# A carried angle added by VectorE to turned gates, in place of a TensorE matmul

## The chip, the cores and the metric

One core of one Trainium2 chip runs the program. The time is the device time of one execution in microseconds (us), given as the median of several executions, with the lowest and highest. A profiled execution is one execution, and its span is some 1.8 us shorter than its own time. In the lines of the profile PE is TensorE, PEld its loading of weights, DVE is VectorE, ACT is ScalarE, POOL is GpSimd, SP is SyncE and SPq its queue. A record is one instruction in the profile. The chain that ended last is the path followed back from the last instruction to whatever released it, step by step.

## The reference, cut to what matters

```python
batch, n_heads, seq, head_dim = 4, 8, 768, 48
n_tokens, d_model, d_ff = 3072, 384, 2048

mag = sqrt(a_re**2 + a_im**2)
a = (a_re + 1j*a_im) * minimum(mag, 0.999) / (mag + 1e-6)      # gates
for t in range(S):                                             # state S, complex
    S = a[t] * S + outer(k[t], v[t])
    y[t] = q[t] @ real(S)
h = x @ w_in                                                   # x: y with heads side by side
out = (h * cos(h)) @ w_out
```

The kernel takes 128 steps as a chunk and two chunks as a group: 24 chunks, 12 groups, six chunks to a batch. Inside a chunk the product of gates over time becomes a running sum of logarithms and of angles, each made by one matmul with a triangular constant. The angle at the end of a chunk is carried into the next one, except where a batch begins (chunks 0, 6, 12, 18).

## The kernel before

`x["tan"]` holds the angles of a group, 128 steps by 2 x 384 columns. The sum `phs` has a second matmul: `last` is zero but for its last row, so it adds the last row of the chunk before, and that row is its carried phase.

```python
def load(g, names, i=None):
    ...
        for i_ in range(G) if i is None else (i,):
            b, c = divmod(g * G + i_, NCH)
            nc.sync.dma_start(out=X[g][name][:, i_],
                              in_=ap[b].rearrange("h (c p) d -> p c h d", p=C)[:, c])

def g_phase(g, i):
    x, n = X[g], g * G + i
    ps = pa.tile([C, DM], F32, tag="a", name="phs")
    first = n % NCH == 0
    matmul(ps, lhsT=turns, rhs=cut(x["tan"], i, 1), start=True, stop=first)
    if not first:
        prev = cut(X[(n - 1) // G]["tan"], (n - 1) % G, 1)
        matmul(ps, lhsT=last, rhs=prev, start=False, stop=True)
    ph = cut(x["tan"], i, 1)
    scalar.copy(out=ph.bitcast(I32), in_=ps)
    vector.tensor_tensor(out=ph, in0=ps, in1=ph.bitcast(I32), op=ALU.subtract)
```

What the steady groups do, in the order in which it is written; the two numbers place a part between the start (0) and the end (1) of a group:

```python
for n in range(2, NG):
    weave((logs(n + 1), 0.0, 0.02), (chunks(n), 0.0, 0.36), (second(n - 1, 0), 0.0, 0.38),
          (prods(n + 1), 0.38, 0.39), (each(g_angle, n + 1), 0.39, 0.4),
          (second(n - 1, 1), 0.4, 0.56), (phases(n + 1), 0.49, 0.51),
          (keys(n + 1), 0.52, 0.7), (first(n), 0.56, 1.0),
          (guarded(n - 1, per) if n > 3 else [], 0.1, 0.9))
```

`first` makes `hp` (x @ w_in), `second` makes `op` (the product with w_out), `chunks` makes `sc`, `sp` and `yp`, the attention of a group. `keys` ends in `moved`, `kT` and `qT`: keys and queries transposed through memory. (Two senses of one word: "turned" queries are these transposed ones; "turned" gates, below, have their rows moved round by one.)

## Time and profile before

| kernel before | value | read from |
|---|---|---|
| time | 720.84 us (720.14 to 721.88) | 3 executions |
| span of the profiled execution | 716.7 us | page |
| TensorE (PE) busy | 688.3 us, 96% | page, part 1 |
| VectorE (DVE) busy | 393.8 us, 55% | page, part 1 |
| period from one `hp` start to the next, the nine of the steady groups | 53.67 to 56.39 us | timeline of PE |

The period varies with a batch's place: two groups out of three have two carried chunks, the third has one.

### The profile page before, as it was taken

The page shows a single profiled execution, that of the slowest core. Times are in us where ns is not written, and L with a number is a line of the kernel's source. Part 1 is how long each engine was busy: PE and PEld are TensorE (multiplying, and loading weights), DVE is VectorE, ACT ScalarE, POOL GpSimd, SP SyncE. Part 2 cuts the span into 40 slices and gives each one's busy share as a digit, 9 for nine tenths or more (in the row PEclk, how much of TensorE's full clock was granted, in tenths as well). Part 3 has the DMA queues.
Part 4 walks back from the last instruction along what each step waited for, and adds up shares of the span by engine and source line. Part 5 has one row for each costly group of instructions (what it writes and reads, how often), then busy time and mean ns, then how long its engine had stood idle before and what let it go on. Part 6 is the DMA issues. An engine that isn't in the chain of part 4 may idle for free.

```text
span 716.7 us, 9385 instructions
## 1 busy us (share of the span) xinstructions
PE 688.3 (96%) x3614; PEld 524.4 (73%) x3614; DVE 393.8 (55%) x548; ACT 386.3 (54%) x690; POOL 26.1 (4%) x45
## 2 busy tenths in 40 slices
PE   6786999999999999999999999999999999999995
PEld 5675776876876876876886876876886786786773
DVE  4889987255455563663663664654645655631110
ACT  6778873564564574484483583474474375342330
POOL 1012000000000000000000000000000000000000
PEclk9979999999999999999999999999999999999998
DMA  9678626625725745646646655556665572272000
GB/s 265 131 226 265 167 56 160 139 55 123 176 49 129 177 133 122 162 138 143 161 137 145 149 145 122 148 155 133 156 154 133 146 163 56 88 173 70 12 0 28
DMA packets 231730, 94.73 MB, mean 132 GB/s; under 512 B 207982, under 2 KB 220145, under 8 KB 231676
## 3 DMA queue, kind: packets, MB, share of 16 engines
q1 hardware_dynamic: 225324, 68.55, 43.5%
q0 software_dynamic: 5632, 25.17, 10.3%
q8 instruction: 30, 0.49, 0.3%
q10 hardware_dynamic: 720, 0.33, 0.2%
q14 instruction: 24, 0.20, 0.1%
HBM read 69.22 MB, written 24.81 MB: 131 GB/s over the span
## 4 chain that ended last, share of the span: by engine, by line
PE 81%; DMA 3%; DVE 3%; SPq 1%; ACT 1%; issue 0%; DVEq 0%
PE op L661 34%; PE hp L661 28%; PE sc L661 6%; PE yp L661 5%; PE phs L661 3%; PE sp L661 3%; DMA qT<-moved 2%; PE lgs L661 2%; DVE w_out L651 1%; SPq L837 1%; DMA raw<-in_moe_w_out_dram 1%; DVE ks L651 0%; DVE qs L651 0%; DMA moved<-tr 0%; DVE tr L651 0%
## 5 line engine op out<-in xcount | busy, mean ns | idle before, releaser
L661 PE MATMUL op<-w_out,gate 128*128 128x384 f32 x768 | 262.8, 489 | 0.7 <-DVE w_out L651 0.7
L661 PE MATMUL hp<-xT,w_in 128*128 128x256 f32 x1152 | 254.3, 382 | 3.9 <-ACT junk L651 3.3
L661 PEld LDWEIGHTS hp<-xT,w_in 128*128 128x128 f32 x1152 | 220.7, 192 | 38.1 <-ACT junk L651 3.7
L661 PEld LDWEIGHTS op<-w_out,gate 128*128 128x128 f32 x768 | 142.3, 190 | 95.1 <-issue 3.7
L651 DVE TENSOR_TENSOR gate<-hp,gate 128x512 f32<-128x512 f32 x96 | 65.5, 683 | 135.4 <-ACT gate L680 135.4
L651 ACT ACTIVATE junk<-hp 128x512 bf16<-128x512 f32 x96 | 57.2, 596 | 81.7 <-DVE gate L651 81.6
L680 ACT ACTIVATE gate<-hp,half_pi_b 128x512 f32<-128x512 f32 x96 | 65.5, 684 | 41.6 <-PE hp L661 41.6
L661 PEld LDWEIGHTS sc<-qT,kT 96*128 96x128 f32 x384 | 47.6, 192 | 11.0 <-issue 4.0
L651 ACT COPY yT<-yp 48x512 f32<-48x512 f32 x44 | 25.4, 577 | 52.7 <-PE yp L661 52.0
L661 PE MATMUL sc<-qT,kT 96*128 96x128 f32 x384 | 49.3, 277 | 2.7 <-DMA qT<-moved 0.9
L651 DVE SCALAR_TENSOR_TENSOR mag<-Q,lg 128x768 f32<-128x768 f32 (+1 forms) x13 | 11.6, 894 | 66.6 <-ACT Q L680 66.6
L651 ACT CAST tan<-phs 128x384 int32<-128x384 f32 x24 | 11.5, 481 | 64.6 <-PE phs L661 64.6
L651 DVE TENSOR_TENSOR atm<-sc,causal 128x512 f32<-128x512 f32 x48 | 32.9, 686 | 19.3 <-PE sc L661 19.3
L651 ACT ACTIVATE ot<-op 128x384 f32<-128x384 f32 x24 | 11.6, 483 | 48.6 <-PE op L661 48.6
L676 ACT ACT_TABLE_LOAD x26 | 33.4, 1283 | 3.5 <-issue 3.1
L661 PE MATMUL yp<-atm,v 128*48 128x128 f32 x352 | 33.5, 277 | 0.0
L651 DVE TENSOR_TENSOR tan<-phs,tan 128x384 f32<-128x384 f32 x24 | 13.4, 557 | 30.9 <-ACT tan L651 30.9
L661 PE MATMUL sp<-v,ks 128*96 128x48 f32 x320 | 29.6, 245 | 0.0
L661 PE MATMUL yp<-qT,state 96*48 96x128 f32 x304 | 29.6, 272 | 0.0
L661 PEld LDWEIGHTS sp<-v,ks 128*96 128x96 f32 x320 | 29.4, 165 | 0.3 <-issue 0.2
L661 PE MATMUL phs<-tan,turns 128*128 128x384 f32 x48 | 19.6, 492 | 4.3 <-ACT tan L680 4.3
L661 PEld LDWEIGHTS yp<-atm,v 128*48 128x48 f32 x352 | 19.3, 122 | 5.6 <-issue 3.3
(93 smaller groups left out, 677.7 us busy)
## 6 DMA issues: line engine op xcount, KB each, us to landing
moved<-tr SPq DMA_DIRECT2D x20, 768.0 KB
raw<-in_moe_w_in_dram POOLq DMA_DIRECT2D x16, 768.0 KB, 6.1
raw<-in_moe_w_out_dram POOLq DMA_DIRECT2D x16, 768.0 KB, 5.1
kT<-moved SPq DMA_DIRECT2D x40, 192.0 KB
qT<-moved SPq DMA_DIRECT2D x10, 768.0 KB
re<-in_a_re_dram SPq DMA_DIRECT2D x24, 192.0 KB
im<-in_a_im_dram SPq DMA_DIRECT2D x24, 192.0 KB
k<-in_k_dram SPq DMA_DIRECT2D x24, 192.0 KB
```

The costliest lines, as they stand in the source:

```text
L651: ins = getattr(self.engine, op)(**kw)
L661: chain(nc.tensor.matmul(out, **kw), "tensor")
L676: chain(nc.scalar.preload_act_table_set(table))
L680: chain(nc.scalar.activation(func=func, **kw))
L837: nc.sync.dma_start(out=X[g][name][:, ds(i * H, n * H), q4], in_=moved[q4])
```

## The change

The gates of group 2 and of the later groups are loaded turned by one row: partition 127 gets step 0 of the chunk, partition p gets step p+1. The triangular constant is turned in the same way, so the sum is the same. What is carried lies in partition 127 of the chunk before, after its sum, and the element that it must be added to lies in partition 127 too. So VectorE can add it in place, on partitions 96 to 127 with a column `carry` that is pi in row 127 and 0 above (the finished sums are kept in units of pi), and the matmul goes. The loads come in parts of 112, 15 and 1 rows. At the same time the order in a group is changed: the decay products come earlier, and the two phase sums stand further apart and earlier.

```diff
+    sums_np = causal_np, np.roll(causal_np, -1, axis=0)
+    carry_np = np.where(step_np == C - 1, np.float32(math.pi), np.float32(0.0))[:, None]
 ...
+            parts = [(0, C, 0)]
+            if name in ("re", "im") and g >= PEG:
+                parts = [(0, C - 16, 1), (C - 16, C - 1, 1)]
+                nc.sync.dma_start(out=tile_[C - 1:C], in_=steps[0:1])
+            for i_ in range(n):
+                for lo, hi, by in parts:
+                    nc.sync.dma_start(out=tile_[lo:hi, i_], in_=steps[lo + by:hi + by, i_])
 ...
+    carry = constant(carry_np, "carry")
 ...
+    def g_carry(g, i):
+        n, some = g * G + i, ds(C - 32, 32)
+        if g >= PEG and n % NCH:
+            head = cut(X[g]["tan"], i, 1)[some]
+            vector.scalar_tensor_tensor(out=head, in0=before(n)[some], scalar=carry[some],
+                                        in1=head, op0=ALU.mult, op1=ALU.add)
 ...  (in g_phase)
+        early = g < PEG and n % NCH
+        if i:
+            g_carry(g, i)
-        matmul(ps, lhsT=turns, rhs=cut(x["tan"], i, 1), start=True, stop=first)
-        if not first:
-            matmul(ps, lhsT=last, rhs=prev, start=False, stop=True)
+        matmul(ps, lhsT=turns[g >= PEG], rhs=cut(x["tan"], i, 1), start=True, stop=not early)
+        if early:
+            matmul(ps, lhsT=last, rhs=before(n), start=False, stop=True)
 ...  (start)
+    sums.append(constant(sums_np[1], "sums_turned", nc.sync))
+    turns.append(constant(sums_np[1] * np.float32(1.0 / math.pi), "turns_turned", nc.sync))
 ...  (steady groups)
-              (prods(n + 1), 0.38, 0.39), (each(g_angle, n + 1), 0.39, 0.4),
-              (second(n - 1, 1), 0.4, 0.56), (phases(n + 1), 0.49, 0.51),
-              (keys(n + 1), 0.52, 0.7), (first(n), 0.56, 1.0),
+              (prods(n + 1), 0.22, 0.24),
+              (second(n - 1, 1), 0.4, 0.56), (phases(n + 1), 0.4, 0.52),
+              (keys(n + 1), 0.49, 0.66), (first(n), 0.56, 1.0),
```

More of the change, by code (lines that the diff above doesn't have):

```diff
@@ L521, in fast_path, with constant @@
     step_np = np.arange(C)
-    sums_np = (step_np[:, None] <= step_np[None, :]).astype(np.float32)
+    causal_np = (step_np[:, None] <= step_np[None, :]).astype(np.float32)
+    sums_np = causal_np, np.roll(causal_np, -1, axis=0)
     last_np = np.zeros((C, C), np.float32)
     last_np[C - 1] = 1.0
-    def constant(array, name):
+    carry_np = np.where(step_np == C - 1, np.float32(math.pi), np.float32(0.0))[:, None]
+    def constant(array, name, queue=nc.scalar):
         t = consts.tile(list(array.shape), F32, name=name)
-        nc.scalar.dma_start(out=t, in_=nc.inline_tensor(array, name=name + "_const").ap())
+        queue.dma_start(out=t, in_=nc.inline_tensor(array, name=name + "_const").ap())
         return t
@@ L548, in load @@
                                      bufs=2 if name == "v" else 1)
-            for i_ in range(G) if i is None else (i,):
-                b, c = divmod(g * G + i_, NCH)
-                nc.sync.dma_start(
-                    out=X[g][name][:, i_],
-                    in_=ap[b].rearrange("h (c p) d -> p c h d", p=C)[:, c])
+            b, c = divmod(g * G + (i or 0), NCH)
+            one, n = i or 0, G if i is None else 1
+            steps = ap[b].rearrange("h (c p) d -> p c h d", p=C)[:, ds(c, n)]
+            tile_ = X[g][name][:, ds(one, n)]
+            parts = [(0, C, 0)]
[5 more added lines that the diff above has]
+                    nc.sync.dma_start(out=tile_[lo:hi, i_], in_=steps[lo + by:hi + by, i_])
     for names in ("re", "im"), ("k", "q"), "v":
@@ L558, in fast_path @@
     ident = constant(np.eye(C, dtype=np.float32), "ident")
-    sums = constant(sums_np, "sums")
-    turns = constant(sums_np * np.float32(1.0 / math.pi), "turns")
+    sums = [constant(sums_np[0], "sums")]
+    turns = [constant(sums_np[0] * np.float32(1.0 / math.pi), "turns")]
     last = constant(last_np, "last")
-    causal = constant(sums_np * np.float32(0.25), "causal")
+    carry = constant(carry_np, "carry")
+    causal = constant(causal_np * np.float32(0.25), "causal")
     tiny_b = scalar_tile(TINY, "tiny_b")
@@ L666, in busy @@
         for _ in range(count):
-            matmul(ps, lhsT=ident, rhs=sums, start=True, stop=True)
+            matmul(ps, lhsT=ident, rhs=sums[0], start=True, stop=True)
     tables = {AF.Ln: "natural_log_exp_and_others", AF.Exp: "natural_log_exp_and_others",
@@ L743, in p_powers @@
         ps = pa.tile([C, DM], F32, tag="a", name="lgs")
-        matmul(ps, lhsT=sums, rhs=cut(x["lg"], i, 1), start=True, stop=True)
+        matmul(ps, lhsT=sums[g >= PEG], rhs=cut(x["lg"], i, 1), start=True, stop=True)
         special(out=cut(x["P"], i, 1), in_=ps, func=AF.Exp)
@@ L775, in p_apply @@
         vector.tensor_tensor(out=u, in0=cut(x["q"], i, n), in1=P, op=ALU.mult)
-    def g_prod(g, i, n):
-        for one in range(i, i + n):
-            p_powers(g, one)
-        p_even(g, i, n)
-        p_apply(g, i, n)
     def g_angle(g, i, n):
@@ L786, in g_angle, with before @@
         special(out=at, in_=at, func=AF.Arctan)
+    def before(n):
+        return cut(X[(n - 1) // G]["tan"], (n - 1) % G, 1)
+    def g_carry(g, i):
[4 more added lines that the diff above has]
+                                        in1=head, op0=ALU.mult, op1=ALU.add)
     def g_phase(g, i):
@@ L791, in g_phase @@
         ps = pa.tile([C, DM], F32, tag="a", name="phs")
-        first = n % NCH == 0
-        matmul(ps, lhsT=turns, rhs=cut(x["tan"], i, 1), start=True, stop=first)
-        if not first:
-            prev = cut(X[(n - 1) // G]["tan"], (n - 1) % G, 1)
-            matmul(ps, lhsT=last, rhs=prev, start=False, stop=True)
+        early = g < PEG and n % NCH
[4 more added lines that the diff above has]
+            matmul(ps, lhsT=last, rhs=before(n), start=False, stop=True)
         ph = cut(x["tan"], i, 1)
@@ L998, in prods @@
     def prods(g):
-        yield from each(g_prod, g)
-        if 0 <= g and g + 1 < NG:
+        if not 0 <= g < NG:
+            return
+        for i in range(G):
+            yield lambda i=i: p_powers(g, i)
+        yield lambda: g_angle(g, 0, G)
+        yield lambda: g_carry(g, 0)
+        yield lambda: (p_even(g, 0, G), p_apply(g, 0, G))
+        if g + 1 < NG:
             yield lambda: load(g + 1, ("k", "q"))
@@ L1081, in fast_path @@
     weave((logs(1), 0.0, 0.1), (convert(into[RAW:]), 0.0, 0.5),
-          (first(0), 0.2, 1.0), (prods(1), 0.55, 0.57), (each(g_angle, 1), 0.58, 0.6),
+          (first(0), 0.2, 1.0), (prods(1), 0.55, 0.58),
           (phases(1), 0.7, 0.8), (keys(1), 0.8, 0.9), (convert(back[:4]), 0.5, 1.0))
@@ L1085, in fast_path @@
     weave((convert(back[4:]), 0.0, 0.3), (second(0, 0), 0.0, 0.65), (over, 0.2, 0.6),
-          (logs(2), 0.3, 0.31), (chunks(1), 0.7, 1.0), (prods(2), 0.85, 0.86),
-          (each(g_angle, 2), 0.86, 0.87))
+          (logs(2), 0.3, 0.31), (chunks(1), 0.7, 1.0), (prods(2), 0.85, 0.87))
     weave((second(0, 1), 0.0, 0.35), (phases(2), 0.0, 0.1), (keys(2), 0.1, 0.4),
```

## The prediction

> **What bounds the kernel now.** I read the page's busy shares and 40 slices first, then the busy time of each engine by stretch, then the waits of TensorE, then the chain that ended last, and last the timeline of one group. Page of the kernel before, parts 1, 2 and 4:
>
> ```profile
> PE 688.3 (96%) x3614; PEld 524.4 (73%) x3614; DVE 393.8 (55%) x548; ACT 386.3 (54%) x690; POOL 26.1 (4%) x45
> ...
> PE   6786999999999999999999999999999999999995
> ...
> PE 81%; DMA 3%; DVE 3%; SPq 1%; ACT 1%; issue 0%; DVEq 0%
> ```
>
> TensorE is full in every slice but the first four and the last. The table by stretch (after the first two columns each engine's busy us) gives the gaps as numbers; these are all 60 us stretches between 120 and 660 in which a gap shows:
>
> ```profile
> 240.00:300.00 60.00, 59.55 (x318) 45.55 (x317) 32.54 (x43) 32.74 (x60) 1.70 (x3) 1.00 0.63 148
> 300.00:360.00 60.00, 59.94 (x312) 45.90 (x311) 31.59 (x42) 34.20 (x64) 1.69 (x3) 1.00 0.66 150
> 360.00:420.00 60.00, 59.55 (x308) 44.97 (x307) 33.63 (x44) 34.60 (x63) 3.20 (x6) 1.00 0.57 134
> ...
> 420.00:480.00 60.00, 59.72 (x343) 45.82 (x343) 32.75 (x44) 34.19 (x60) 1.81 (x4) 1.00 0.59 151
> ...
> 600.00:660.00 60.00, 59.51 (x300) 43.94 (x301) 25.09 (x35) 23.80 (x47) 1.62 (x3) 1.00 0.41 109
> ```
>
> Gaps: 0.45 + 0.06 + 0.45 + 0.28 + 0.49 = 1.73 us in 540 us. So in the middle of the kernel each us of TensorE work taken away should be a us of time, as long as nothing that feeds TensorE was only just in time. Something is. The chain that ended last (start, length, what) shows one group's end:
>
> ```profile
> 609.12 1.29 PE phs L661 x4
> 610.41 2.58 PE op L661 x8
> 612.99 1.30 PE phs L661 x4
> ...
> 631.25 6.69 DMA qT<-moved
> ...
> 638.07 1.13 PE sc L661 x8
> ```
>
> After the second phase sum (end 614.29) TensorE has 2.58 us of op and 20.72 us of hp to do, 23.3 us, and would start sc at 637.6. The turned queries land at 637.94: cast, subtract, sine, four products, two transposes and three transfers take 23.65 us from the end of the phase sum. Four other groups miss or meet it as narrowly; those five sc starts hold the 1.73 us. Both lengths matter below.
>
> [...] 128x384 on VectorE takes 545 to 559 ns. [...] I estimate the new 32x384 operation at 0.55 us too. [...] an f32 matmul is two instructions in the trace and the chain gives 1.29/4 = 0.322 us for each. [...]
>
> **The change part by part.** *Removed.* The matmul of `last` with the previous phases. From the tile view of the phase sums, before:
>
> ```profile
> L661 PE MATMUL phs<-tan,turns x48: 486/486/590, 20.0 to 613.2; 128*128 128x384 f32 x48
> ...
> L661 PE MATMUL phs<-tan,last x40: 486/486/590, 22.0 to 613.8; 128*128 128x384 f32 x40
> ```
>
> 40 records are 20 matmuls. Chunks 0 to 3 keep theirs (three of them, chunk 0 has none); chunks 6, 12 and 18 begin a batch and never had one. So 24 - 4 - 3 = 17 go, as the instruction order of the two builds confirms (20 against 3). Each is two records of 0.322 us in the chain; the 486 ns is latency of a pipelined instruction, and 17 x 2 x 0.486 would overstate it. 17 x 0.645 = **11.0 us**, all after 108 us, where TensorE is full.
>
> *Added on VectorE.* 17 operations of 0.55 us, 9.4 us on an engine that is 55% busy. Half of them (first chunk of each group) stand among the decay products, long before they are needed. The other half lie between the two phase sums of a group, where TensorE has only eight op records to do. Timeline before, 553 to 558 us:
>
> ```profile
> 554.62 2.74 PE L661 MATMUL op<-w_out,gate 128*128 128x384 f32 x8
> 554.87 0.48 ACT L651 CAST tan<-phs 128x384 int32<-128x384 f32 x1 [3.36 <-PE phs L661]
> 555.38 0.56 DVE L651 TENSOR_TENSOR tan<-phs,tan 128x384 f32<-128x384 f32 x1 [1.31 <-ACT tan L651]
> ...
> 557.20 0.81 PE L661 MATMUL phs<-tan,turns 128*128 128x384 f32 x2
> ```
>
> Before, only the `last` matmul at 557.84 needed the subtraction. Now the whole second sum needs subtraction and addition: 555.94 + 0.55 + about 0.2 to signal = 556.7, against 557.2. It fits by half a us, if VectorE is idle when the cast ends. In the steady groups it is: the decay products now stand before the sums and I work out that VectorE is through with them about 21 us into the group, while the first sum starts at 25. In the first changed group (around 109 us) it is not. There the products run until 111.8 already, the new operation in their midst adds 0.55, so subtraction and addition end near 113.2 instead of a sum start at 112.5, and the first sum waits some 0.3 us for its own addition. **About +1.0 us**, once.
>
> *Moved.* The second sum of a steady group is now followed by 16 op records, not 8. From its end to sc there are 5.16 + 20.72 = 25.9 us for a path of 23.65 us, and the first gate no longer stands between the two transposes. So the late queries come about 2 us early and the 1.73 us vanish: **-1.7 us**. Had the order stayed, the missing 1.29 us per group would have been lost to that wait from the second group on; the reordering is what lets the removal count.
>
> *Loads.* For each of the ten later groups ten gate transfers instead of four, with the same bytes. Their issue takes the SyncE queue some 0.4 to 0.5 us each (the four now take 1.02 + 0.99), so about 3 us more per group, at a place where the queue then waits: before, it stood idle from 543.0 to 544.1 and more. They are needed one group (54 us) later. Two more constants of 64 KB go out at the start, where the page shows 226 to 265 GB/s: 128 KB is 0.5 us of it, and as that stretch ends in a wait for converted weights I put **+0.3 us**.
>
> Sum: -11.0 - 1.7 + 1.0 + 0.3 = -11.4 us. 720.8 - 11.4 = **709.4 us**, -1.6%.
>
> **The rivals.** *The new chain between the sums ends last.* If the addition lands a us later than I think (more signalling time, VectorE not idle), ten groups lose up to 1 us each and the gain is near 1 to 3 us: 715 to 719. For it speaks the margin of 0.5 us; against it, in every steady group I looked at, VectorE's idle time before the subtraction is over 1 us, and the products are now moved ahead of it. Losses of 0.2 us in each group would make 711.5.
>
> *The input of hp comes late.* The transfers of yT to xT now stand in the SyncE queue behind the decay row, k and q. I estimate q issued 22.4 us into the group, then x and xT; in the group at 113 us the kernel before has this order already: x at 114.94, xT at 118.33, hp at 122.1 without a wait, so 7.2 us suffice. Now there are some 11. Only heavy traffic of the many 192-byte runs could eat the 4 us left. It would cost perhaps 1 us a group: 719.
>
> *The wait for the queries stays the bound.* Then the time falls by less than the matmuls' worth: if it were still 23.65 us after a sum that is not earlier, nothing would be won. The moved op records speak clearly against it; I give it little.
>
> *More than the sum.* TensorE has no more gaps to give between 120 and 690. To pass 2% (706.4) another 3 us would have to come from the first 95 us, where the order of ScalarE and VectorE is unchanged in the two builds. Unlikely.
>
> **Range and chances.** The matmuls' 11.0 us is firm, the 1.7 us nearly. The uncertain terms are the start and the first changed group (0 to 2 us), small waits for the addition (0 to 3 us), and 0.9 us by which runs of the same kernel differ (720.14 to 721.88). So 706.8 to 713.0, skewed upwards. Faster by over 2%: 0.06; within 2%: 0.92; slower: 0.02.
>
> **What would show it right or wrong.** Right: 6 records of phs<-tan,last instead of 40; TensorE busy near 677 us; 17 VectorE operations of 32x384 at 0.55 us; phs x2 with 0.65 us in the chain; no DMA qT in TensorE's waits; a period of two steady groups shorter by 1.3 us for each with two removed sums. Wrong: TensorE waiting for VectorE's tan before phs in many groups (first rival), or hp waiting for xT (second), or for re and im late in the log steps. If the 32-row operation takes clearly less than 0.55 us, the first rival loses more ground.

## The result, and the profile after

The changed kernel takes **710.53 us** (710.01 to 711.91, 4 executions), beside 721.12 us (720.14 to 721.88, 4 executions) for the kernel before on the same chip. The ratio is 0.9857, with a 95% interval of 0.9837 to 0.9876. (A ratio is the mean time of one kernel's fast runs over that of the other's of the same rounds, so it is not quite the ratio of the medians quoted.) The prediction was 709.4 us with a range of 706.8 to 713.0.

Page of the changed kernel, parts 1, 2 and 4 (busy us and share; granted clock in 40 slices; shares of the chain that ended last):

```profile
PE 679.7 (96%) x3580; PEld 519.9 (73%) x3580; DVE 402.9 (57%) x565; ACT 388.9 (55%) x690; POOL 26.1 (4%) x45
...
PEclk8989899999999999999999999999999999999999
...
PE 84%; DVE 6%; DMA 4%; ACT 4%; issue 1%; SPq 0%; DVEq 0%
```

The clock row of the kernel before:

```profile
PEclk9979999999999999999999999999999999999998
```

TensorE has 34 records and 8.6 us less, VectorE 17 operations and 9.1 us more. The clock row is the first sign of something that the prediction did not weigh: of the first five slices three are below 90% of full clock, where the kernel before has one. The views by tile, first of the phase sums and then of the new column:

```profile
L673 PE MATMUL phs<-tan,last x6: 486/538/847, 23.8 to 81.3; 128*128 128x384 f32 x6
```

```profile
L663 DVE SCALAR_TENSOR_TENSOR tan<-tan,carry x17: 616/618/619, 112.9 to 603.2; 32x384 f32<-32x384 f32 x17
```

Six records are left of 40, and 17 operations have come. Each takes 0.618 us, not the 0.55 us of the prediction. The table by stretch of the changed kernel (second column: length and PE busy), for two of the stretches in which the kernel before had gaps of 0.45 and 0.49 us:

```profile
240.00:300.00 60.00, 60.00 (x324) 46.57 (x323) 33.87 (x46) 34.46 (x64) 1.69 (x3) 1.00 0.67 154
...
600.00:660.00 60.00, 59.74 (x302) 44.01 (x301) 20.73 (x28) 18.91 (x38) 1.62 (x3) 1.00 0.47 109
```

The chain of the changed kernel in a steady group (start, length, what), which answers to the last group's chain shown of before:

```profile
547.10 0.65 PE phs L673 x2
...
550.32 0.65 PE phs L673 x2
550.97 5.16 PE op L673 x16
556.13 20.72 PE hp L673 x96
576.85 0.89 PE sc L673 x8
```

Each sum is now two records of 0.322 us in place of four, and the scores follow `hp` at once. From the end of the second sum to `sc` are 5.16 + 20.72 us, as the prediction had it. In the timeline of the same group the addition lies where it was expected:

```profile
548.29 0.56 DVE L663 TENSOR_TENSOR tan<-phs,tan 128x384 f32<-128x384 f32 x1 [4.13 <-ACT tan L663]
...
548.89 0.62 DVE L663 SCALAR_TENSOR_TENSOR tan<-tan,carry 32x384 f32<-32x384 f32 x1
...
550.16 0.81 PE L673 MATMUL phs<-tan,turns_turned 128*128 128x384 f32 x2
```

It ends at 549.51, 0.65 us before the sum that needs it, and the sum waits for nothing. What TensorE does wait for after 100 us is this, first in the kernel before, then in the changed one (us in total, times, longest):

```profile
PE sc L661 <- DMA qT<-moved: 0.9, 2, 0.5
PE sc L661 <- issue: 0.7, 2, 0.4
```

```profile
PE hp L673 <- DMA xT<-x: 1.1, 2, 0.8
PE phs L673 <- DVE tan L663: 0.8, 1, 0.8
...
PE phs L673 <- PE yp L673: 0.5, 1, 0.5
```

(The line left out is a wait of 0.6 us for the last converted weights, at 100 us. It belongs to the start, and the kernel before has the same wait at 95 us.) The waits for the turned queries are gone. In their place stand three in the first changed group (0.46 us before the first sum, 0.80 before the second, 0.81 before `hp`) and one of 0.26 us at 611 us. The wait of the first sum is put down to `yp`, but VectorE's addition ended at 113.55 us and the sum's weights began to load at 113.62, so it is the addition that it waited for.

To see where the time went I cut each profiled execution in three: start to the second group's first `hp`, from there to the last group's first `hp`, and from there to the end. "Carried matmul" tells whether `last` is used after group 1.

| kernel | carried matmul | to 2nd `hp` | middle | end | span |
|---|---|---|---|---|---|
| before | yes | 121.9 | 545.95 | 48.83 | 716.7 |
| before, again (e1) | yes | 123.1 | 548.15 | 49.03 | 720.3 |
| before, 32 bytes moved (e11) | yes | 123.3 | 546.32 | 49.14 | 718.8 |
| order alone (e2) | yes | 122.6 | 542.94 | 48.88 | 714.4 |
| order, loads in parts (e14) | yes | 125.2 | 543.04 | 48.04 | 716.3 |
| changed, old order (e3) | no | 125.6 | 537.70 | 47.81 | 711.1 |
| changed | no | 127.4 | 533.90 | 47.92 | 709.2 |
| changed, 32 bytes more (e10) | no | 127.2 | 533.82 | 47.80 | 708.8 |
| changed, three costs removed (e12) | no | 124.2 | 533.82 | 48.01 | 706.0 |

The middle is 12 us shorter, as the matmuls and the order promise. The start is 5.5 us longer and the end 0.9 us shorter, and neither was predicted so. The start is the part in which executions of one kernel differ: the kernel before needs 121.9 and 123.1 us in two profiled executions.

### The profile page after: what moved, and what is told of

Same layout as the page of the kernel before. It is cut to its first block, busy times and chain, and to the rows that moved or that the text cites. A ratio compares the mean times of both kernels' runs of the same rounds, so it can differ in the third digit from the quotient of the medians.

```text
span 709.2 us, 9429 instructions
## 1 busy us (share of the span) xinstructions
PE 679.7 (96%) x3580; PEld 519.9 (73%) x3580; DVE 402.9 (57%) x565; ACT 388.9 (55%) x690; POOL 26.1 (4%) x45
## 3 DMA queue, kind: packets, MB, share of 16 engines
q0 software_dynamic: 5632, 25.17, 10.5%
## 4 chain that ended last, share of the span: by engine, by line
PE 84%; DVE 6%; DMA 4%; ACT 4%; issue 1%; SPq 0%; DVEq 0%
PE hp L673 33%; PE op L673 31%; PE sc L673 6%; PE yp L673 5%; PE sp L673 3%; PE phs L673 2%; PE lgs L673 2%; DMA xT<-x 2%; DVE w_out L663 1%; DVE w_in L663 1%; DMA raw<-in_moe_w_out_dram 1%; DVE tan L663 1%; ACT raw L663 1%; PE yr L673 1%; DMA im<-in_a_im_dram 1%
## 5 line engine op out<-in xcount | busy, mean ns | idle before, releaser
L663 DVE STREAM_TRANSPOSE tr<-ks 128x1536 f32<-128x1536 f32 x10 | 22.4, 2236 | 0.0
L663 DVE STREAM_TRANSPOSE tr<-qs 128x1536 f32<-128x1536 f32 x10 | 22.4, 2236 | 0.0
```

Source lines behind the costliest of these rows:

```text
L663: ins = getattr(self.engine, op)(**kw)
```

## The experiments

Eleven kernels ran. All gave a correct result. Those of one call share a chip and the runs of the kernel before, whose median was 721.07 to 721.82 us there.

**e1, the kernel before once more.** No edit; one look, to learn how far two profiled executions of one program differ.

> The kernel before, unchanged, for a second profile of its start. Its first profile was of an execution of 718.55 us, below all of its timed runs (720.14 to 721.88), so the 7.5 us between the two profiled spans (716.7 and 709.2) understates the change by some 3 us. Theory A (the granted clock of the first 100 us varies between executions): this profile has the first op matmuls that wait for w_out nearer to 97 or 98 us than to the 95.5 us of the first, with a lower granted clock in 36 to 80 us than 0.88, and the part from the first hp of the second group to the end unchanged at 588 us. Theory B (the 4.2 us by which the changed kernel's start was late are all due to the change): the start is again at 95.5 us and the span is again near 716.7 us.

It took 722.05 us with a span of 720.3. The wait for the last weights ended at 96.69 us instead of 95.5, so a part of the difference does come from the start. But the part from the second `hp` to the end did not stay the same: it was 597.2 us instead of 594.8 (the 588 us of the expectation fits neither profile), and the waits for the turned queries were 3.3 us in all instead of 1.7. The profile of before that the prediction rests on was of an execution faster than all the timed ones, and it showed half of the waits that the second profile shows. What is typical two profiles can't say.

**e2, the order alone.** The new order of a group, with the matmul, the gates and the loads of before. (Not shown: the order inside the decay products and the places in the first two groups are also those of the changed kernel.)

```diff
-              (prods(n + 1), 0.38, 0.39), (each(g_angle, n + 1), 0.39, 0.4),
-              (second(n - 1, 1), 0.4, 0.56), (phases(n + 1), 0.49, 0.51),
-              (keys(n + 1), 0.52, 0.7), (first(n), 0.56, 1.0),
+              (prods(n + 1), 0.22, 0.24),
+              (second(n - 1, 1), 0.4, 0.56), (phases(n + 1), 0.4, 0.52),
+              (keys(n + 1), 0.49, 0.66), (first(n), 0.56, 1.0),
```

> The kernel before with the new order of the groups' work alone (decay products, phase sums and stacks earlier), gates not turned, all 20 matmuls with last kept. My sum gave the order 1.7 us, the waits for the turned queries: 719.3, -0.25%, no DMA qT in TensorE's waits. Rival: the order is worth more, because it also changes which weights follow which on TensorE: then -0.4% or more. Rival: the order costs time by itself, since xT now comes behind k and q in the SyncE queue: then the time is that of before or longer, with TensorE's hp waiting for DMA xT in several groups.

It took 717.42 us (716.04 to 719.41), ratio 0.995 (0.9927 to 0.9974): 3.6 us below the mean of before (1.9 to 5.3), twice what the prediction gave the order. TensorE waits for nothing after 100 us. Two things are seen that can make up the factor: the second profile of before (e1) has more of these waits than the first, and each wait costs more than its idle time. The chain of the kernel before, shown in the prediction, has the eight `sc` records after the late queries at 1.13 us. The same place in this run's chain:

```profile
635.96 0.89 PE sc L661 x8
```

So 0.24 us are lost after each wait as well. Five such starts are 1.2 us (the fifth waited only 0.06 us), and with 1.67 us of idle time (0.45 + 0.45 + 0.28 + 0.49) that is 2.9 us, against 3.0 us between the two middles in the table. In these profiles that leaves 0.1 us for the rival of the expectation, that another order of weights on TensorE helps by itself.

**e3, the change with the old places.** The gates turned, the matmul gone, but the sums, products and keys of the steady groups where they were.

```diff
-              (prods(n + 1), 0.22, 0.24),
-              (second(n - 1, 1), 0.4, 0.56), (phases(n + 1), 0.4, 0.52),
-              (keys(n + 1), 0.49, 0.66), (first(n), 0.56, 1.0),
+              (prods(n + 1), 0.38, 0.4),
+              (second(n - 1, 1), 0.4, 0.56), (phases(n + 1), 0.49, 0.51),
+              (keys(n + 1), 0.52, 0.7), (first(n), 0.56, 1.0),
```

> The changed kernel with the phase sums, products and stacks of the steady groups put back to the places they had before; 17 matmuls gone, additions on VectorE kept. Theory 1, of my prediction: without the reordering the missing 1.29 us per group is lost again to the wait for the turned queries from the second group on, so nine groups lose 1.29 us: about 722, no gain. Theory 2, which I now hold: the path to the queries starts at the second sum, which itself moves earlier with TensorE, so only the 0.3 to 0.6 us by which that path is longer than TensorE's work behind the sum is lost, plus what the sums wait for the additions: 10 groups x 0.3 to 1 us, so 713 to 719, with TensorE's waits naming DMA qT or DVE tan.

It took 712.99 us (710.15 to 713.39), ratio 0.9876 (0.985 to 0.9902): 8.9 us gained without the new places, at the lower edge of theory 2. TensorE's wait for the queries, in this run:

```profile
PE sc L673 <- DMA qT<-moved: 2.3, 3, 0.8
```

One more wait of 0.9 us before `sc`, with no releaser that the profile shows, belongs to it. That is no more than what before has (1.7 and 3.3 us in its two executions). The prediction's sentence that without the reordering the gain would be lost is refuted. The reason follows from where the work lies: the removed matmuls lie *ahead of* the point from which the path to the queries starts, the end of the second sum. Their removal moves the start of that path and TensorE's own arrival at `sc` forward together, so the race between them does not change. (In this run's group at 555 us the queries land 23.3 us after the subtraction of the second sum starts, 554.56 to 577.83 us. In the group of before that the prediction shows it is 23.1 us, 614.83 to 637.94.)

**e9, the addition three times.** The second chunk's addition is followed by two of the same kind that add zero.

```diff
+            for _ in range(2 if i else 0):
+                vector.scalar_tensor_tensor(out=head, in0=before(n)[some], scalar=nothing[some],
+                                            in1=head, op0=ALU.mult, op1=ALU.add)
```

> The changed kernel with the addition before the second phase sum of each group done three times (twice with a column of zeros, so the result stays). Each measured 0.617 us; in the profile after, the addition of a steady group ends at 549.51 and the second sum starts at 550.16, so some 0.55 us are left. Theory: the addition is hidden in this margin, and two more pass it by 0.7 us in each of ten groups, more in the first one: 7 to 9 us longer than the changed kernel, ratio 0.995 to 0.998, with TensorE's phs waiting for DVE tan in all ten groups. Rival: the addition is not on the way of the second sum's start at all (TensorE gets there later for its own work): less than 2 us longer.

It took 717.42 us (715.06 to 718.18), ratio 0.995 (0.9922 to 0.9977), about 6.9 us more than the changed kernel:

```profile
PE phs L674 <- DVE tan L664: 7.5, 10, 2.1
```

All ten groups wait now, the first for 2.1 us, the other nine for 0.54 to 0.63 us each. Two more operations of 0.617 us are 1.23 us; less the wait, 0.60 to 0.69 us of margin stood there. The first rival was well placed, and the change stays clear of it by about one operation.

**e6, the addition over all 128 rows.** To find out why the operation takes 0.62 us.

```diff
-        n, some = g * G + i, ds(C - 32, 32)
+        n, some = g * G + i, ds(0, C)
```

> The changed kernel with the addition over all 128 rows instead of 32. My estimate of 0.55 us for 32x384 was low: it measured 0.617 us. Theory A: the 0.06 us more come from the per-row column that is read as scalar, and the rows cost nothing: 0.617 us again with 128 rows, and the same time. Theory B: it comes from starting at row 96, or from the 32 rows: then 0.557 us with 128 rows, like the other operations of 384 columns. Theory C: rows cost: clearly more than 0.62.

709.45 us, and by tile

```profile
L663 DVE SCALAR_TENSOR_TENSOR tan<-tan,carry x17: 607/619/620, 111.5 to 601.6; 128x384 f32<-128x384 f32 x17
```

Four times the rows cost nothing (0.619 against 0.618 us). So the extra 0.06 us over a 128x384 operation of two tensors (0.557 us) is not in the rows. Nor is it in the form alone. The changed kernel has operations of this form with a number instead of a column, and they are no slower than those of two tensors: its early ones over 128x384 took 0.551 to 0.558 us, the later ones over 128x768 0.95 us, as two tensors alone do. What is left is the column of scalars.

**e4, the new constants later.** The two turned constants and `carry` are loaded behind the queries of the third group, on SyncE's queue.

```diff
-    carry = constant(carry_np, "carry")
-    sums.append(constant(sums_np[1], "sums_turned", nc.sync))
-    turns.append(constant(sums_np[1] * np.float32(1.0 / math.pi), "turns_turned", nc.sync))
+    def late():                      # called in the weave of group 1, behind loads[2, "q"]
+        last_load = loads[2, "q"]
+        sums.append(constant(sums_np[1], "sums_turned", nc.sync, last_load))
+        turns.append(constant(..., "turns_turned", nc.sync, last_load))
+        carry = constant(carry_np, "carry", nc.sync, last_load)
```

> The changed kernel with the three new constants (two of 64 KB, and the column of 128 words that was on ScalarE's queue before the causal mask) fetched on the SyncE queue behind the second group's k and q, after some 80 us, instead of at the start. Theory A: these fetches delay the start (the second im lands 0.8 us later, after which TensorE idles longer and runs at a lower clock): 1 to 2 us come back, ratio 0.983 to 0.984 against 0.9857 of the changed kernel, and ScalarE's first Ln starts at 7.7 us again instead of 8.5. Theory B: the late start is the chance of the clock: ratio 0.985 to 0.986, no change.

It took 709.28 us (707.83 to 711.37), ratio 0.983 (0.9807 to 0.9854), which is where theory A put it, but its interval overlaps that of the changed kernel (0.9837 to 0.9876). The loads at the start are no faster: 205 GB/s between 4 and 8 us against 202, and ScalarE's first logarithm starts at 8.42 us against 8.49 (7.68 in before). So the bytes of the constants are not what slows the start. Nor are the longer idle time and the lower clock of the expectation special to the changed kernel. In the first 36 us TensorE is busy for 25.77 us at a granted clock of 0.95 in before and for 24.24 us at 0.91 in the changed kernel, but also for 24.62 us at 0.91 in e1, the unchanged program; here it is 25.17 us at 0.95. One thing did go: with `carry` on ScalarE's queue SyncE waited 1.1 us for the first load of `re` before it issued the fourth gate load, and now it does not. This run's profile also has more waits of `hp` for the rows of x: 2.1 us in all against 1.1, one of them 1.00 us at 611 us, where the changed kernel has 0.26.

**e10 and e11, 32 bytes.** What else could make the same loads slower? `carry` is one column, and in the compiled program it takes 32 bytes, so the tile of the gates begins at byte 71136 of each partition instead of 70080 (the two other constants add 512 bytes each): an odd multiple of 32 in place of a multiple of 64. The two runs cross this: e10 is the changed kernel with 32 bytes of filling more, e11 is the kernel before with 32 bytes of filling.

```diff
+    consts.tile([C, 8], F32, name="pad")
```

> The changed kernel with 32 unused bytes behind the new column of constants, so that all tiles that come after it start at a multiple of 64 bytes in SBUF again, as in the kernel before (the gates' tile at 71168 instead of 71136; before: 70080). Nothing else differs. Theory A: the 32-byte shift makes the loads of 192-byte runs slower, which is why all kernels with the new constants move only 202 to 205 GB/s between 4 and 8 us, where those without move 232 to 236, also when the constants are fetched late: then 230 GB/s or more come back, the DMA share of the first 36 us falls from 0.97 to 0.87 or less, and the time falls by 1 to 2 us, ratio 0.983 to 0.984 against 0.9857. The wait of hp for xT may shrink as well. Theory B: the start is slow for the extra fetches or by chance: 202 to 205 GB/s stay and the ratio stays within 0.985 to 0.987.

> The kernel before with 32 unused bytes at the same place, so that its load tiles start at an odd multiple of 32 bytes (the gates' tile at 70112). No other change. Theory A (the shift slows the loads): about 200 GB/s between 4 and 8 us instead of 232 to 236, a DMA share near 0.95 in the first 36 us, ScalarE's first Ln at 8.4 us instead of 7.7 to 7.9, and 1 to 3 us longer in time, also because the path to the turned queries has no slack here: ratio 1.001 to 1.005. Theory B: nothing differs, ratio 0.999 to 1.001.

The table by stretch between 4 and 8 us (last three columns: clock, DMA share, GB/s), of the changed kernel, of e10 and of e11:

```profile
4.00:8.00 4.00, 3.76 (x18) 3.79 (x19) 0.56 (x1) 2.42 (x4) 0.00 (x0) 1.00 1.39 202
```

```profile
4.00:8.00 4.00, 3.97 (x21) 4.00 (x22) 0.56 (x1) 2.87 (x6) 0.52 (x2) 1.00 1.24 231
```

```profile
4.00:8.00 4.00, 3.65 (x17) 3.68 (x18) 0.56 (x1) 1.96 (x4) 0.00 (x0) 1.00 1.37 204
```

The filling brings the changed kernel back to 231 GB/s (236 in before) and takes the kernel before down to 204. The first logarithm follows: 7.88 us in e10, 8.52 in e11. Over the first 36 us the DMA share (the time that packets took, over the time of 16 engines; it can pass 1, as in the three lines above) is 0.83 in e10 and 0.86 in before, against 0.97 in the changed kernel and 0.96 in e11. This cause of the slower loads is shown in both directions. (Other profiles whose tiles lie at a multiple of 64, those of e12 and e14, have 228 and 226 GB/s.) In time it is small: e10 took 708.92 us (707.87 to 710.57), ratio 0.9826 (0.9803 to 0.9849), and e11 took 722.86 us (720.61 to 723.93), ratio 1.0025 (1.0004 to 1.0047), so 1.8 us with an interval of 0.3 to 3.4. (e11's profiled execution was the fastest of its six, so its row in the table does not show this loss.) The pairs of runs show 202 against 231 GB/s and 204 against 236, an eighth to a seventh less. By which mechanism the place of a tile slows the loads into it is not shown.

**e14, the order alone with loads in parts.** As e2, but the gates of the later groups come in 112, 15 and 1 rows, not turned.

```diff
-            for i_ in range(G) if i is None else (i,):
-                nc.sync.dma_start(out=X[g][name][:, i_], in_=...[:, c])
+            parts = [(0, C)]
+            if name in ("re", "im") and g >= PEG:
+                parts = [(0, C - 16), (C - 16, C - 1)]
+                nc.sync.dma_start(out=tile_[C - 1:C], in_=steps[C - 1:C])
+            for i_ in range(n):
+                for lo, hi in parts:
+                    nc.sync.dma_start(out=tile_[lo:hi, i_], in_=steps[lo:hi, i_])
```

> The kernel with the order alone (matmul kept, gates not turned), but with its gates from the third group on loaded in parts of 112, 15 and 1 rows. Theory A (the ten loads per group cost nothing, and the shorter stretch at the end comes with the SyncE instructions): time 716.0 to 717.5, 0.5 to 1 us below the order alone (717.42 there), stretch from the last hp to the end 47.9 us, periods as in the order alone (53.67, 54.82, 55.71). Theory B (the end belongs to PE's or VectorE's program, the loads cost nothing): 717.4, stretch 48.9. Theory C (the extra loads cost time, for instance as a wait for the turned queries behind them in the queue): periods longer than 53.67, 54.82, 55.71 by some tenths, with a wait for qT or xT in TensorE's list.

It took 717.8 us (716.05 to 718.66), ratio 0.994 (0.9913 to 0.9968), not apart from e2. Two effects of opposite sign stand in its profile. TensorE's list has one entry:

```profile
PE hp L667 <- DMA xT<-x: 0.7, 1, 0.7
```

This is the wait of the first changed group, and it is here without any turning: the ten loads in place of four cause it. And the end is 48.04 us, as in the kernels without the matmul, against 48.88 in e2. So the shorter end comes with the loads in parts, and not with the matmuls or the additions. Which part of the program does it is not shown: the trace has 53 records of SyncE more than e2's (525 against 472), but also 15 more of VectorE and 19 more of ScalarE, none of them counted as work. After the last output's store is issued, the traces show five instruction fetches in before, e1, e2 and e11, and four in e14 and in every turned kernel. Whether the one fetch less saves the 0.9 us is not shown.

**e5, two parts of 127 and 1 rows.** The changed kernel without the split into 112 and 15 rows.

```diff
-                parts = [(0, C - 16, 1), (C - 16, C - 1, 1)]
+                parts = [(0, C - 1, 1)]
```

> The changed kernel, but the turned gates come in two parts, 127 rows and 1 row, instead of 112, 15 and 1. Theory A[...]: a load of 127x8 runs goes through one engine of 16; the four such loads of a group are then 4064 runs in a row on a single engine. The changed kernel's trace has about 75 ns of one engine for a run of 192 bytes (the start: 8 loads of 1024 runs on 16 engines), which makes 76 us for one load and over 300 us for a group's, so the logs wait for re and im in every group and the kernel takes far over 1500 us. Theory B (the parts do not matter on this chip): all waits as in the changed kernel, 709 to 712 us. A second thing to read: after the last output of the turned kernels the profile has four instruction fetches, in the kernels that are not turned five, and the stretch from the last start of hp to the end is 47.8 to 48.0 against 48.8 to 49.1 us. If the number of SyncE instructions sets that, this kernel (16 SyncE rows more than the one with the order alone, where the changed one has 76 more) may fall back to 48.8; if it is PE's or VectorE's, it stays at 47.9.

1124.47 us. TensorE's longest entry, the table by stretch, and SyncE's issue of one such load, in this run:

```profile
PE hp L673 <- DMA xT<-x: 351.1, 9, 41.1
```

```profile
560.00:570.00 10.00, 0.00 (x0) 0.00 (x0) 0.00 (x0) 0.00 (x0) 0.00 (x0) 0.50 0.08 16
```

```profile
634.31 11.85 SPq L561 DMA_DIRECT2D im<-in_a_im_dram  x1
```

Theory A holds in kind: a load of 127 rows (195 KB) runs at 16 GB/s with a DMA share of 0.08, where one engine of 16 would be 0.06, and takes 11.9 us. Four of them per group hold the queue, the rows of x stand behind them, and each group is 40 us longer. My size was wrong by a factor of six: I had put 75 ns to a run of 192 bytes, an estimate from the start of the changed kernel's trace, and 11.9 us / 1016 runs is 11.7 ns. So 112 + 15 + 1 is what makes turned loads usable here: 710.53 us in place of 1124.47. By which rule the rows of a load are shared out among the engines is not shown. The end is 47.81 us here too, with only 16 SyncE records more than in e2.

**e12, three side costs removed.** The changed kernel with e10's filling, with e4's late constants, and with k and q of the fourth group loaded behind the rows of x in the first changed group.

```diff
+    consts.tile([C, 8], F32, name="pad")
 ...  (late() as in e4)
-        if g + 1 < NG:
+        if g + 1 < NG and g != 2:
             yield lambda: load(g + 1, ("k", "q"))
 ...
-            yield lambda: load(g + 2, ("v",))
+            yield lambda: load(g + 2, ("k", "q", "v") if g == 1 else ("v",))
```

> The changed kernel with its three side costs taken away together: 32 bytes of filling so that the gates' tiles lie at a multiple of 64 again, the three new constants loaded behind the queries of the third group, and k and q of the fourth group loaded after the rows of x in the first changed group, so that xT does not stand behind them. Theory A: these costs are what is left of the start and the first changed group: no wait of hp for xT there (0.8 us), a first Ln at 7.9 instead of 8.5 us, so 1.4 to 2.2 us below the changed kernel: 708.0 to 709.1, ratio to the kernel before 0.981 to 0.9825. Theory B (the differences of the start between executions swamp it): not to be told from the filling alone, 708.9 us and ratio 0.9826.

It took **707.56 us** (706.7 to 707.77), ratio 0.9799 (0.9778 to 0.982), the fastest kernel and a little below what theory A gave. Its interval lies below the changed kernel's (0.9837 to 0.9876). The wait of `hp` in the first changed group is gone, and the first logarithm is at 7.87 us. The place of k and q is what takes that wait away, for it stands in e10 (0.99 us) and in e4 (0.95 us), which have the two other edits. The waits of the two sums there are left (0.45 and 0.80 us).

## Why the prediction was right, and where its steps were not

**The matmuls, -11.0 us: right.** From e2 to the changed kernel the steady periods go from 55.71 to 54.41, from 54.81 to 53.53 and from 53.67 to 53.03 us: 1.30, 1.28 and 0.64 us for two, two and one removed matmul. Each is worth 0.645 us, as the chain said, and not the 0.97 us of its records, which overlap: two records of 0.486 us take 0.81 us in the timeline.

**The addition hides: right, with its size off.** It takes 0.618 us instead of 0.55, and e9 shows a margin of 0.6 to 0.7 us where the prediction worked out 0.5. The 0.2 us that it added for signalling, an estimate read from no trace, was too much: in the first changed group the sums' weights begin to load 0.05 and 0.07 us after an addition. And its "half of them" is 7 of the 17 additions among the products and 10 between the sums.

**The order, -1.7 us: mis-sized, -3.6 us measured (e2).** The term counted the idle time in one profile. It left out 0.24 us of slower scores after each wait (e2), and the second profile has twice the idle time (e1).

**"The reordering is what lets the removal count": refuted** by e3, which gains 8.9 us with the old places.

**The first changed group, +1.0 us: right mechanism for two waits, and a third one missed.** The timeline of the changed kernel shows VectorE at the products when the second sum's path needs it:

```profile
115.79 0.94 DVE L663 TENSOR_TENSOR mag<-q,lg 128x768 f32<-128x768 f32 x1
116.66 0.55 DVE L663 TENSOR_TENSOR tan<-phs,tan 128x384 f32<-128x384 f32 x1
117.24 0.62 DVE L663 SCALAR_TENSOR_TENSOR tan<-tan,carry 32x384 f32<-32x384 f32 x1
117.91 0.30 PEld L673 LDWEIGHTS phs<-tan,turns_turned 128*128 128x128 f32 x2 [1.42 <-DVE tan L663]
```

The cast ended at 115.05, but the subtraction came at 116.66. This wait (0.80) and that of the first sum (0.46) make 1.26 us. The second rival then takes 0.81 us more: the rows of x were issued at 119.75, and `hp` at 127.38 had to wait for them,

```profile
119.75 1.41 SPq L953 DMA_DIRECT2D x<-yT  x2
...
127.38 2.86 PE L673 MATMUL hp<-xT,w_in 128*128 128x256 f32 x12 [0.81 <-DMA xT<-x]
```

where the prediction thought 7.2 us to be enough and had 11 in hand. In a steady group they are 8.8 (547.19 to 555.97), and here 7.6. It is 2.1 us in all. Without the ten loads (e2) the wait is not there, with them alone it is (e14), and with k and q behind the rows of x it goes away (e12).

**The start, +0.3 us: the wrong term.** The 128 KB of constants are not to be seen in the rate (e4). The place of the tiles, moved by 32 bytes, costs 1.8 us (0.3 to 3.4, e11).

**The end: not in the prediction.** It gives 0.85 us back, and e14 lays that to the program with the loads in parts.

The sum with the measured terms is -11.0 - 3.6 + 2.1 + 1.8 - 0.85 = -11.6 us; the medians differ by -10.6. About 1 us stays open, and since the -3.6 and the 1.8 are each known only to some 1.6 us either way, the runs can't place it. In the first 100 us an execution also loses time to the granted clock, which differs between executions. The same stretch in the changed kernel and in e12 (clock in the third column from the end):

```profile
76.00:80.00 4.00, 4.00 (x12) 3.14 (x11) 1.76 (x3) 1.94 (x4) 0.00 (x0) 0.57 1.10 230
```

```profile
76.00:80.00 4.00, 4.00 (x18) 3.16 (x17) 1.96 (x4) 3.30 (x7) 0.00 (x0) 1.00 1.12 223
```

TensorE counts as busy in both, but it gets 12 records done against 18. What sets the granted clock is not shown. It differs between two executions of one program: from 40 to 60 us it is 0.74 in before and 0.83 in e1, from 60 to 72 us 1.00 and 0.86. Idle time alone does not decide it: from 72 to 76 us TensorE stands idle for 1.41 us in the changed kernel, 1.61 us in e11 and 2.23 us in e3, at clocks of 0.58, 1.00 and 1.00. Between 72 and 80 us a drop stands in eight of the nine profiles whose gates are loaded in parts (all but e3; e14 too, which has nothing turned), and in none of the four others (before, e1, e2, e11: 1.00 from 72 to 76 and from 76 to 80 us). In seven of the eight the lower clock of those two stretches is 0.50 to 0.79; in e5 the drop is read from the first sum, whose first matmul takes 1.65 us at 74.02 us, as in the changed kernel, against 0.91 us in before. So the loads in parts, and not the turning, seem to favour it; how they would, no run shows, and the timed runs of e14 and e2 are too close to tell what it costs. e10's profiled execution had it and was the slowest of its five (710.57 us), which may be why its first column in the table shows no gain.

One sign of being right was missed: TensorE's busy time is 679.7 us and not near 677. The slow matmuls between 72 and 80 us can account for that, since e3, without the drop, has 677.7.

So the total was right for two reasons. The large term was read from the chain and was exact. The errors in the small ones were of both signs: the order gave 1.9 us more than predicted, and first changed group, start and end together cost 1.75 us more. That these cancel is luck.

## What to carry to other kernels

Here TensorE was full (96% busy), and a removed matmul was worth its length in the chain, 0.645 us. It counted with the old places too (e3: 8.9 us gained), for it lay ahead of the start of the next critical path; ask on which side of that start it lies before fearing that a wait will eat it. One profile is one execution (the waits for the queries were 1.7 us in one and 3.3 us in the other): have a second look at the unchanged kernel before a small wait is sized from it, and add what runs slower after each wait (0.24 us here). A new small constant can move every later tile (here by 32 bytes, worth 1.8 us in e11), so compare the addresses of load tiles before and after, and look at the queue in which new loads stand ahead of old ones (0.81 us of wait before `hp` here).
